# Two attention and two gated MLP layers on one core: gate and up weights copied inside DRAM into 4 KB rows and loaded from the copies

## The chip, the cores and the metric

The kernel runs on one core of one Trainium2 chip. The metric is the device time of one execution in microseconds (us), the median of several runs.

## The reference

Four layers are applied to one sequence x of 2048 tokens and 1024 features (bfloat16): attention, MLP, attention, MLP, each on a layer-normalised input and with its result added to x. Attention is linear, with 32 heads of 32 features. Cut to what matters:

```python
q, k, v = split(layernorm(x) @ wqkv)
phi = lambda t: where(t > 0, t + 1, exp(t)) + 1e-6
kv = einsum("bhsd,bhse->bhde", phi(k), v);  z = sum over tokens of phi(k)
x = x + ((phi(q) @ kv) / (phi(q) . z + 1e-6)) @ wo            # attention
gate, up = layernorm(x) @ W_gate, layernorm(x) @ W_up          # 1024 x 3584 each
x = x + ((gate * (gate > 0)) * up) @ W_down                    # MLP
```

## The kernel before

The tokens stand in 16 tiles of 128, in four quarters of four tiles. An attention layer (`layer_A`) goes through these stages on TensorE: projections to k and q, quarter by quarter (line 506; a unit is one token tile by 512 columns, eight matmuls of 128x512); the attention token products, in which phi(k) is multiplied with the tokens themselves (`m_products`, line 588); the small products with the value weights; and the output products (line 789). In the first layer, four quarters of projections take TensorE from 6 us to 104 us, and the token products follow until about 150 us.

Each projection unit writes one PSUM bank. ScalarE (lines 448 and 449) and VectorE (line 452, the join) empty it. The units rotate over a pool `ps` of four banks; in the first three quarters of layer 0 every third unit uses one of the two banks of `ps3`; in the last quarter only `ps` is used. A unit needs its token tile normalised by VectorE and transposed by a DMA (line 423, `xnT`), which the queue of SyncE (SP) issues.

Into the first layer's projections the kernel puts preparations for the MLP: 1 MB blocks of `W_down` are loaded (line 1218, tiles `wd`), VectorE makes four differences of each (line 1230), and SP stores them (line 1232, `td`).

An MLP layer (`layer_B`) runs in two chunks of 1024 tokens. Layers 1 and 3 are MLPs, so the chunks are (1,0), (1,1), (3,0), (3,1). Each chunk goes through 14 units u of 256 columns of `W_gate` ("g") and `W_up` ("u"). For each unit `load_gu` brings 128 partitions x 8 rows x 256 columns of bfloat16 of each of the two, so 1024 pieces of 512 bytes, 512 KB. Seven products instead of eight are made from blocks of them (line 1301). The differences of weight blocks that this takes are made in chunk (1,0) by `make_gu`, stored in DRAM as `tgu` in rows of 4 KB, and loaded again in the other three chunks (line 1202).

The weights go through a ring of five SBUF tiles (`_Ring`): a load is issued when the tile that it takes has come free. `_Later` holds jobs that are due at a count of steps (`later.at(delay, job)`); each unit of TensorE work is a step. Within blocks marked `manual_schedule` the named engines keep the order of the code. For all other engines a scheduler of the framework places each instruction, from its dependencies and its own estimate, so an instruction may stand on its queue far ahead of where the code names it. SP's queue is not among those named in the block that holds the token products (VectorE and GpSimd are).

SP issues its DMAs in order; an instruction that waits holds all that stand behind it. ScalarE's queue issues a few loads too, among them the first q weights in the first microseconds.

Of the kernel before, what the change touches and what calls it, by code (L numbers as in the profile page):

```python
# [11 lines left out]
BF16 = mybir.dt.bfloat16  # L12
F16 = mybir.dt.float16
PSUM = bass.MemoryType.PSUM
P = 128
NW = 512
# [7 lines left out]
class _Ring:  # L24


    def __init__(self, nc, slot, depth):
        self.nc, self.slot, self.depth = nc, slot, depth
        self.plan, self.tiles, self.loaded = [], {}, 0
# [63 lines left out]
class _Net:  # L93
    def __init__(self, tc, ctx, x_d, wqkv_d, wo_d, wg_d, wu_d, wd_d, out_d):
        nc = tc.nc
        self.tc, self.nc = tc, nc
        _, S, D = x_d.shape
        self.S, self.D = S, D
        self.ST, self.KT = S // P, D // P
        self.G = D // P  # L100
        self.F = wg_d.shape[1]
        self.FT = self.F // P
        self.NQ = self.ST // QT
        self.x_v = x_d.rearrange("b (st p) d -> p (b st) d", p=P)
        self.o_v = out_d.rearrange("b (st p) d -> p (b st) d", p=P)
        self.wqkv_v = wqkv_d.rearrange("(kt p) n -> p kt n", p=P)
        self.wo_v = wo_d.rearrange("(kt p) n -> p kt n", p=P)
        self.wgu_v = {"g": wg_d.rearrange("(kt p) f -> p kt f", p=P),
                      "u": wu_d.rearrange("(kt p) f -> p kt f", p=P)}
        self.wd_v = wd_d.rearrange("(u h p) n -> p h u n", p=P, h=2)  # L110
        self.U = self.F // (2 * P)

        pool = lambda name, bufs, **kw: ctx.enter_context(tc.tile_pool(name=name, bufs=bufs, **kw))
        self.const = pool("const", 1)
        self.xres = pool("xres", 1)
        self.big = pool("big", 16)
        self.ep = pool("ep", 7)
        self.small = pool("small", 4)
        self.ps = pool("ps", 4, space=PSUM)
        self.ps3 = pool("ps3", 2, space=PSUM)  # L120
        self.kvp = pool("kvp", 1, space=PSUM)


        self.spill = pool("spill", 1, space=bass.MemoryType.DRAM)
        self.NS = self.ST // 2
        self.ring = _Ring(nc, self.slot, 5)
        self.tgu = {(w, u): self.spill.tile([P, 4, NW], F16, name=f"t{w}{u}")
                    for w in "gu" for u in range(self.U)}
        self.td = self.spill.tile([P, 4, self.U, NW], F16, name="td")
        self.tw = {n: self.spill.tile([P, 8, NW], F16, name=f"t{n}") for n in ("q0", "q1", "k0", "k1")}  # L130
        self.dd = {p: self.spill.tile([P, 7, self.U // 2, NW // 2], F16, name=f"dd{p}") for p in self.DEEP}
        self.gi = {(m, u): self.spill.tile([P, 4, 2, 2, P], F16, name=f"gi{m}_{u}")
                   for m, first in ((5, 2), (6, 3)) for u in range(first, self.U - 1, 2)}
        self.inner = {}
        self.later = _Later()
        self.phi_lag = 0

        from concourse.masks import make_identity
        self.ident = self.const.tile([P, P], BF16, name="ident")
        make_identity(nc, self.ident[:, :])  # L140
        self.ones = self.const.tile([P, P], BF16, name="ones")
        nc.vector.memset(self.ones, 1.0)
        self.mean = 2.0 ** -11
        assert self.S == 2 ** 11
        self.eps6 = self.const.tile([P, 1], F32, name="eps6")
        nc.vector.memset(self.eps6, 1e-6)
        self.eps5 = self.const.tile([P, 1], F32, name="eps5")
        nc.vector.memset(self.eps5, 1e-5)
        self.xall = self.xres.tile([P, self.ST, D], F32, name="x")
        self.x = [self.xall[:, t, :] for t in range(self.ST)]  # L150
        self.acc = self.const.tile([P, 2 * self.ST], F32, name="acc")

        self.xb = [x[:, D // 2:D].bitcast(BF16) for x in self.x]
        self.xnT, self.xn, self.pk, self.slabs, self.xs = {}, {}, {}, {}, {}
        self.away = [self.spill.tile([P, D], F32, name=f"away{t}") for t in range(self.ST)]
# [324 lines left out]
    def layer_A(self, l, last_ln):  # L480
# [34 lines left out]
        def k_unit(q, j, c, between=None):  # L515
            t = q * QT + j
            pk = self.pk_home(l, t)
            self.phi(project(f"k{c}", q, j, between), pk[:, c * NW:(c + 1) * NW])
            later.at(1 + (10 if self.phi_lag else 0), lambda: k_sum(t, slice(c * NW, (c + 1) * NW)))
# [126 lines left out]
        def q_unit(sc, j, c, lag=None):  # L646
            if c == 0 and (sc, j) not in pq_of:
                a = self.slot(f"pq{l}_{sc}", [P, QT, D])
                for i in range(QT):
                    pq_of[sc, i] = a[:, i, :]  # L650
            pq = pq_of[sc, j]
            self.phi(project(f"q{c}", sc, j), pq[:, c * NW:(c + 1) * NW])
            if c == H - 1 and lag is not None:
                later.at(lag, lambda: z_mult(sc, j))
# [212 lines left out]
        def column_major(f, q):  # L867
            return [lambda j=j, c=c: f(q, j, c) for c in range(H) for j in range(QT)]
# [33 lines left out]
        if l == 0:  # L902
            first = self.head_units(lambda *a: k_unit(0, *a), lambda *a: q_unit(0, *a), *steps)
        else:
            first = column_major(k_unit, 0)
# [10 lines left out]
        else:  # L916
            run(first)
            k = iter(row_major(k_unit, 1))
# [22 lines left out]
        with self.tc.manual_schedule(engines={mybir.EngineType.DVE, mybir.EngineType.Pool}):  # L941
            q3 = row_major(q_unit, self.NQ - 1)
            out0 = column_major(out_unit, 0)
            bring = self.bring_back if l else self.load_x
            ring.load_to(ring.index((l, "v1")) + 1)
            m_products(q3.pop(0))
            q3.insert(0, lambda: None)
            later.at(1, lambda: self.behind(ring.last, bring, range(self.NS)))
            for t in range(self.NS, self.ST - QT, 2):
                later.at(10 + t, lambda t=t: self.behind(self.last_turn, bring, (t, t + 1)))  # L950

            def with_fold(u, i):
                return lambda: (u(), fold_wo(i // 2) if i % 2 == 0 else None)

            run(q3[:2])
            run([with_fold(u, i) for i, u in enumerate(q3[2:] + out0[:1])])
            run(out0[1:3])
            ring.free_slowly((l, "o0"), later, 2)
            for i in range(11, self.ST):
                later.at(1 + 3 * (i - 11), lambda i=i: z_mult(*divmod(i, QT)))  # L960
            self.ln_later(last_ln, 0, 2, 2, 2)
            run(out0[3:])
            for sc in range(1, self.NQ - 1):
                if sc == 1:
                    for j in range(QT):
                        self.ln_at(2 * j + 2, last_ln, QT + j, 2)
                        later.at((11 if l else 12, 13, 15, 16)[j], lambda j=j: self.sums_x(last_ln, 0, j))
                if sc == 2 and l:
                    for j in range(QT):
                        later.at(11 + j, lambda j=j: q_turn(self.NQ - 1, j))  # L970
                    for t in range(self.ST - QT, self.ST):
                        later.at(3 + t, lambda t=t: self.behind(self.last_turn, bring, (t,)))
                if sc == 1 and l == 0:
                    for w, n in (("g", 3), ("u", 11)):
                        later.at(n, lambda w=w: self.behind(
                            self.last_x, lambda w: self.make_gu(ring.get((last_ln, 0, w, 0)), w, 0), (w,)))
                run(row_major(out_unit, sc))
            self.pairs = out_pairs(self.NQ - 1)
            self.turns = [] if l else [lambda j=j: q_turn(self.NQ - 1, j) for j in range(QT)] + [
                lambda t=t: self.behind(self.last_turn, bring, (t,)) for t in range(self.ST - QT, self.ST)]  # L980
# [213 lines left out]
    def sums_gu(self, t):  # L1194
        return t[:, 4:8, :].bitcast(F16).rearrange("p t (k f) -> p t k f", f=P)

    def load_gu(self, t, w, u, first, d):
        self.nc.sync.dma_start(out=self.raw_gu(t),
                               in_=self.wgu_v[w][:, :, u * 2 * P:(u + 1) * 2 * P])
        if not first:  # L1200
            b = slice(1, 4, 2) if 6 in d else slice(5 in d, 4)
            self.nc.sync.dma_start(out=t[:, 4:8, :][:, b, :].bitcast(F16), in_=self.tgu[w, u][:, b, :])
# [609 lines left out]
```

## Time and profile before

| | |
|---|---|
| median of 3 runs | 1438.24 us (1438.23 to 1438.44) |
| profiled execution, its own time | 1439.99 us |
| its span, first to last instruction | 1437.9 us |
| TensorE (PE) matmul busy | 1427.1 us, 99% |
| VectorE (DVE) / ScalarE (ACT) / GpSimd (POOL) busy | 1045.2 / 623.3 / 309.3 us |
| queue of SP: bytes, share of 16 DMA engines | 313.57 MB, 73.1% |
| loads of gate and up weights | 56 + 56, 512 KB each |

The profiled execution is 1.75 us above the median, and 2.1 us of it lie around its span. The busy time of PE is a model (matmuls overlap their ends), so waits of PE are read from the idle time before its instructions. The DMA share is the mean busy share of the core's 16 DMA engines. Packets of one engine overlap a little, so a saturated stretch shows a share above 1. The granted clock was 1.000 over the span.

### The profile page before, as it was taken

To read this page: it belongs to the slowest core of one execution; us is meant where nothing else is said; L and a number is where in the kernel's file an instruction comes from. 1 tells how busy PE (TensorE), PEld (TensorE's weight loads), DVE (VectorE), ACT (ScalarE), POOL (GpSimd) and SP (SyncE) were. 2 spreads that over 40 slices of the span, in tenths; PEclk is the share of its full clock that TensorE was granted. 3 is DMA by queue.
4 is the path that set the end of the run, shared out by engine and by line. 5 is a ranking of instruction groups with operands and counts; after the bars stand their busy time and mean duration, and the time that the engine had idled before them with its cause. 6 is when DMAs were issued, how large, how long until landed. Compare 5 with 4: busy or idle time off the path is not lost.

```text
span 1437.9 us, 21394 instructions
## 1 busy us (share of the span) xinstructions
PE 1427.1 (99%) x7720; PEld 739.7 (51%) x7748; DVE 1045.2 (73%) x2013; ACT 623.3 (43%) x1143; POOL 309.3 (22%) x220
## 2 busy tenths in 40 slices
PE   9999999999999999999999999999999999999998
PEld 4444444444455444545654444445554565555557
DVE  7978698778685666558778886866766864766895
ACT  7872564333325244332058725733443433444301
POOL 1453860010100011110032477510111011111102
PEclk9999999999999999999999999999999999999999
DMA  9950787898559999966983218998878699975575
GB/s 286 240 162 8 172 209 202 278 335 288 200 192 294 323 367 345 291 216 199 302 277 93 70 22 234 287 274 262 268 225 294 228 304 335 274 229 174 193 260 183
DMA packets 367865, 337.74 MB, mean 235 GB/s; under 512 B 110032, under 2 KB 327760, under 8 KB 366736
## 3 DMA queue, kind: packets, MB, share of 16 engines
q1 hardware_dynamic: 359184, 313.57, 73.1%
q10 hardware_dynamic: 7136, 18.88, 3.4%
q0 software_dynamic: 1440, 3.93, 0.7%
q8 instruction: 60, 0.98, 0.3%
q14 instruction: 45, 0.37, 0.1%
HBM read 246.87 MB, written 64.82 MB: 217 GB/s over the span
## 4 chain that ended last, share of the span: by engine, by line
PE 91%; DVE 3%; DMA 2%; ACT 2%; SPq 1%; issue 1%; ACTq 0%; DVEq 0%
PE ps L506 11%; PE yu L1301 9%; PE yg L1301 9%; PE xg L1301 6%; PE xu L1301 6%; PE dy L1447 6%; PE dx L1447 5%; PE i L1154 5%; PE ps L789 4%; PE zu L1301 3%; PE zg L1301 3%; PE my L588 3%; PE dyT L1489 2%; PE mv L588 2%; PE mx L588 2%; PE dy L1489 2%
## 5 line engine op out<-in xcount | busy, mean ns | idle before, releaser
L1301 PEld LDWEIGHTS <-w 128*128 128x128 f16 (+1 forms) x2768 | 270.4, 98 | 297.2 <-issue 4.6
L506 PE MATMUL ps<-w,xnT 128*128 128x512 bf16 x768 | 169.9, 380 | 0.6 <-ACT xnT L361 0.2
L1381 POOL TENSOR_TENSOR h<-m5u,m5g 128x512 f16<-128x512 f32 x28 | 37.1, 1326 | 425.3 <-DVE m5u L1377 252.5
L506 PEld LDWEIGHTS <-xnT 128*128 128x128 bf16 x768 | 74.4, 98 | 90.3 <-issue 1.8
L1301 PE MATMUL xg<-xnT,w 128*128 128x512 f16 x448 | 115.5, 379 | 0.0
L1301 PE MATMUL xu<-xnT,w 128*128 128x512 f16 x448 | 115.0, 380 | 0.0
L1489 PEld LDWEIGHTS <-h 128*128 128x128 f16 x1008 | 98.6, 98 | 12.9
L1381 POOL TENSOR_TENSOR h<-c22u,c22g 128x512 f16<-128x512 f32 x28 | 36.0, 1285 | 289.8 <-DVE c22u L1377 247.8
L1447 PEld LDWEIGHTS <-h 128*128 128x128 f16 x616 | 60.3, 98 | 71.8 <-issue 0.3
L1301 PE MATMUL yu<-s,w 128*128 128x512 f16 x376 | 96.5, 379 | 0.5 <-DVE zu L1357 0.5
L1301 PE MATMUL yg<-s,w 128*128 128x512 f16 x376 | 96.9, 379 | 0.0
L449 ACT ACTIVATE e<-e,eps 128x512 f32<-128x512 f32 x128 | 91.0, 720 | 3.2
L736 POOL TENSOR_TENSOR kvc<-pq,kvc 128x1024 f32<-128x1024 bf16 x32 | 78.5, 2452 | 53.1 <-DVE den L741 32.8
L789 PE MATMUL ps<-T,pqT 128*128 128x512 bf16 x374 | 83.0, 380 | 0.5
L1328 DVE TENSOR_TENSOR h<-yu,r 128x512 f16<-128x512 f32 x56 | 38.6, 690 | 53.8 <-PE yu L1301 53.8
L1325 ACT ACTIVATE r<-yg 128x512 f32<-128x512 f32 x56 | 33.4, 597 | 101.3 <-PE yg L1301 101.3
L527 POOL TENSOR_TENSOR kvc<-kvc,slab 128x512 f32<-128x512 f32 x46 | 57.2, 1249 | 75.9 <-DVE slab L452 72.7
L1447 PE MATMUL dx<-w,h 128*128 128x512 bf16 x327 | 72.5, 380 | 0.5
L448 ACT ACTIVATE e<-ps 128x512 f32<-128x512 f32 x92 | 54.2, 590 | 28.4 <-PE ps L506 27.9
L1154 PEld LDWEIGHTS <-x 128*128 128x128 f16 x504 | 49.3, 98 | 33.5 <-issue 1.9
L1325 ACT ACTIVATE r<-zg 128x512 f32<-128x512 f32 x56 | 32.9, 587 | 76.7 <-PE zg L1301 76.7
L748 POOL TENSOR_TENSOR pq<-pq,den 128x1024 bf16<-128x1024 bf16 x32 | 61.1, 1909 | 6.8 <-DVE den L743 6.8
(286 smaller groups left out, 2630.6 us busy)
## 6 DMA issues: line engine op xcount, KB each, us to landing
w<-in_B_W_gate_dram SPq DMA_DIRECT2D x56, 512.0 KB, 6.4
w<-in_B_W_up_dram SPq DMA_DIRECT2D x56, 512.0 KB, 6.0
w<-ddT SPq DMA_DIRECT2D x21, 896.0 KB, 6.4
w<-td SPq DMA_DIRECT2D x18, 896.0 KB, 5.0
w<-dd SPq DMA_DIRECT2D x18, 896.0 KB, 5.9
x<-away SPq DMA_DIRECT2D x30, 512.0 KB, 7.5
away<-x SPq DMA_DIRECT2D x24, 512.0 KB, 8.1
w<-in_B_W_down_dram SPq DMA_DIRECT2D x12, 896.0 KB, 6.1
```

What stands on the lines that cost most here:

```text
L449: self.last_exp = nc.scalar.activation(out=e, in_=e, func=ACT.Exp, scale=-1.0, bias=self.eps6[:, 0:1])
L506: nc.tensor.matmul(by_row(ps), lhsT=self.xnT[l, l_q][:, kt, j * P:(j + 1) * P], rhs=w[:, kt, :].rearrange("p (b i d) -> p i b d", i=R, d=H ...
L588: nc.tensor.matmul(banks[j], lhsT=A(i)[:, j * P:(j + 1) * P], rhs=B(i), start=start and i == 0, stop=i == NS - 1, skip_group_check=True)
L736: nc.gpsimd.tensor_tensor(out=prod, in0=pq_of[sc, j], in1=zrow, op=ALU.mult)
L748: nc.gpsimd.tensor_tensor(out=heads(pq), in0=heads(pq), in1=den[:, :].unsqueeze(2).to_broadcast([P, D // HD, HD]), op=ALU.mult)
L789: nc.tensor.matmul(ps, lhsT=pqT[sc][:, g, j * P:(j + 1) * P], rhs=T[g // 4][:, g % 4, n2 * NW:(n2 + 1) * NW], start=(g == 0), stop=(g == G ...
L1154: nc.tensor.matmul(b[:, w, :], lhsT=B[p][:, w, k, :], rhs=A[p][:, k, :], start=start and w == 0 and k == 0, stop=k == 1, skip_group_check= ...
L1301: nc.tensor.matmul(ps, lhsT=W[w][m][:, k, :], rhs=A[m][:, k, :], start=start and k == 0, stop=k == 3, skip_group_check=True)
L1325: self.last_relu = nc.scalar.activation(out=out, in_=ps, func=ACT.Relu)
L1381: nc.gpsimd.tensor_tensor(out=h[:, 3, :], in0=V["u"], in1=V["g"], op=ALU.mult)
L1447: nc.tensor.matmul(banks[j], lhsT=A(k)[:, j * P:(j + 1) * P], rhs=w[:, i, :], start=start and k == 0, stop=k == self.U - 1, skip_group_che ...
L1489: nc.tensor.matmul(out, lhsT=A[i // 2][:, i % 2, j * P:(j + 1) * P], rhs=B[m][:, i, :], start=start and i == 0 and j == 0, stop=i == NK - ...
```

## The change

Each of the 28 blocks of gate and up weights gets a tile `wc` in DRAM, and `lay_again` issues one DMA from DRAM to DRAM for it on SP's queue: 1024 pieces of 512 bytes are read at the stride of the weight matrix and written one behind the other, so that a partition's eight pieces make one row of 4 KB. The calls stand at the start of the token products: units 0 to 6 in layer 0, units 7 to 13 in layer 2. `load_gu` takes the copy where the code has already named it, except for the first two units of chunk (1,0): that is units 2 to 6 in chunk (1,0), units 0 to 6 in (1,1), and all 14 in (3,0) and (3,1), 80 of the 112 loads. The other loads are as before.

```diff
+        self.wc = {(w, u): self.spill.tile([P, 4, NW], BF16, name=f"c{w}{u}")
+                   for u in range(self.U) for w in "gu"}
+        self.relaid = set()
...
             ring.load_to(ring.index((l, "v1")) + 1)
+            self.lay_again(range(self.U // 2, self.U) if l else range(self.U // 2), 1, 2)
             m_products(q3.pop(0))
...
+    def lay_again(self, units, first, step):
+
+        def lay(w, u):
+            self.nc.sync.dma_start(out=self.wc[w, u][:, :, :].rearrange("p a (b f) -> p (a b) f", f=2 * P),
+                                   in_=self.wgu_v[w][:, :, u * 2 * P:(u + 1) * 2 * P])
+            self.relaid.add((w, u))
+
+        for n, u in enumerate(units):
+            for k, w in enumerate("gu"):
+                self.later.at(first + (2 * n + k) * step, lambda w=w, u=u: lay(w, u))
+
     def load_gu(self, t, w, u, first, d):
-        self.nc.sync.dma_start(out=self.raw_gu(t),
-                               in_=self.wgu_v[w][:, :, u * 2 * P:(u + 1) * 2 * P])
+        if (w, u) in self.relaid and not (first and u < 2):
+            self.nc.sync.dma_start(out=t[:, 0:4, :], in_=self.wc[w, u][:, :, :])
+        else:
+            self.nc.sync.dma_start(out=self.raw_gu(t),
+                                   in_=self.wgu_v[w][:, :, u * 2 * P:(u + 1) * 2 * P])
```

The order of matmuls on PE and of the work on GpSimd is the same in both kernels. On VectorE a few rows near 50 us change places, on ScalarE four. SP's queue has 28 DMAs more, and the scheduler puts them as follows. The first place is the head of SP's queue, while the first token tiles are loaded, normalised and transposed (`w` with a number: weights of the projections; `xnT_0`, `xnT_1`: transposed tokens of the first and second quarter). Before:

```order
L463 DMA x<-in_A_x_dram 128x1024
L40 DMA w_176<-in_A_wqkv_dram 128x4x512
L463 DMA x<-in_A_x_dram 128x1024
L423 DMA_TRANSPOSE xnT_0_189<-x 128x8x128 x2
L463 DMA x<-in_A_x_dram 128x1024 x10
L423 DMA_TRANSPOSE xnT_1_439<-x 128x8x128
```

And in the changed kernel, from the last of these loads of x on (`cg`, `cu`: the copies of gate and up blocks):

```order
L466 DMA x<-in_A_x_dram 128x1024
L1204 DMA cg_109<-in_B_W_gate_dram 1024x1x256
L1204 DMA cu_110<-in_B_W_up_dram 1024x1x256
L1204 DMA cg_111<-in_B_W_gate_dram 1024x1x256
L1204 DMA cu_112<-in_B_W_up_dram 1024x1x256
L426 DMA_TRANSPOSE xnT_0_217<-x 128x8x128
L1204 DMA cg_113<-in_B_W_gate_dram 1024x1x256
L426 DMA_TRANSPOSE xnT_0_217<-x 128x8x128
L466 DMA x<-in_A_x_dram 128x1024 x10
L1204 DMA cu_114<-in_B_W_up_dram 1024x1x256
L1204 DMA cg_115<-in_B_W_gate_dram 1024x1x256
L1204 DMA cu_116<-in_B_W_up_dram 1024x1x256
```

Five copies stand ahead of the loads of x that the second quarter needs, and eight ahead of its first transposition. The second place is further down SP's queue, at the last block of `W_down` that the first layer's projections prepare (`wd_1111` before, `wd_1139` after). Before:

```order
L423 DMA_TRANSPOSE xnT_3_883<-x 128x8x128 x2
L1218 DMA wd_989<-in_B_W_down_dram 128x4x1024
L1232 DMA td<-wd_840 128x2x512 x4
L423 DMA_TRANSPOSE xnT_3_883<-x 128x8x128 x2
L1232 DMA td<-wd_989 128x2x512 x4
L1218 DMA wd_1111<-in_B_W_down_dram 128x4x1024
L40 DMA w_1222<-in_A_wqkv_dram 128x8x512
```

And in the changed kernel:

```order
L426 DMA_TRANSPOSE xnT_3_911<-x 128x8x128 x2
L1250 DMA td<-wd_1017 128x2x512 x4
L1204 DMA cu_126<-in_B_W_up_dram 1024x1x256
L1204 DMA cg_127<-in_B_W_gate_dram 1024x1x256
L1204 DMA cu_128<-in_B_W_up_dram 1024x1x256
L1204 DMA cg_129<-in_B_W_gate_dram 1024x1x256
L1204 DMA cu_130<-in_B_W_up_dram 1024x1x256
L1204 DMA cg_131<-in_B_W_gate_dram 1024x1x256
L1204 DMA cu_132<-in_B_W_up_dram 1024x1x256
L1204 DMA cg_133<-in_B_W_gate_dram 1024x1x256
L1236 DMA wd_1139<-in_B_W_down_dram 128x4x1024
L40 DMA w_1250<-in_A_wqkv_dram 128x8x512
```

Of the 28 copies, those of layer 2 included, 25 stand ahead of this last `wd` load: 17 ahead of the third block of `W_down`, eight between the stores of the fourth and the load of the fifth. The last three come behind it, ahead of the transpositions of q at 140 us.

## The prediction

> **What bounds the kernel now.** I read the page first, then the work by stage.
>
> ```profile
> span 1437.9 us, 21394 instructions
> PE 1427.1 (99%) x7720; PEld 739.7 (51%) x7748; DVE 1045.2 (73%) x2013; ACT 623.3 (43%) x1143; POOL 309.3 (22%) x220
> ```
> ```profile
> 0.00:20.00 20.00, 17.95 (x85) 7.84 (x86) 13.17 (x31) 12.34 (x25) 3.84 (x10) 1.00 0.87 268
> 1420.00:1437.90 17.90, 13.98 (x129) 12.28 (x126) 6.59 (x12) 1.24 (x3) 3.99 (x6) 1.00 0.21 64
> ```
>
> (The second fence: stretch, its length, busy time of PE, weight loads, DVE, ACT and POOL, granted clock, DMA share, GB/s.) PE is idle for 1437.9 - 1427.1 = 10.8 us. Of these 2.05 lie in the first 20 us and 3.9 in the last 18, where no gate or up load is waited for, so at most 4.8 us are left for all waits on loads in the MLPs. The longest of them:
>
> ```profile
> 469.90 6.20 DMA xnT<-xnb
> 491.65 9.00 DMA w<-tu
> ```
> ```profile
> 479.52 1.02 PE L1301 MATMUL vg<-s,w 128*128 128x512 f16 x4 [0.35 <-DVE x L1460]
> 500.69 0.61 PE L1301 MATMUL vu<-s,w 128*128 128x512 f16 x2 [1.11 <-DMA w<-tu]
> ```
>
> The first two rows are the chain of waits at the start of chunk (1,1): it runs through a transposition that takes 6.2 us to land and a weight load that takes 9.0 us, both behind a full queue. The other two are what PE lost there, 0.35 and 1.11 us.
>
> Next comes the stage into which the copies go.
>
> ```profile
> 0.00:91.30 91.30, 89.25 (x416) 40.13 (x417) 74.91 (x137) 70.59 (x135) 29.52 (x30) 1.00 0.87 248
> 5.00:10.00 5.00, 4.30 (x30) 2.08 (x30) 4.25 (x11) 2.63 (x8) 0.00 (x0) 1.00 1.08 359
> 105.00:140.00 35.00, 34.89 (x162) 15.84 (x162) 28.84 (x74) 12.01 (x20) 11.55 (x5) 1.00 0.00 1
> 9.05 51.33 PE L506 MATMUL ps<-w,xnT 128*128 128x512 bf16 x237
> ```
>
> From 9 us on PE runs without a wait, and the DMAs that feed it are at a share of 0.87 over 91 us, where 1.08 is a full queue. The idle DMA time comes later: 35 us at a share of 0.00 under the token products. The queue order shows that the copies don't stand there, but in the first 91 us.
>
> **The change: the later loads.** 80 loads of 512-byte pieces become loads of 4 KB rows. Prices of 512 KB:
>
> ```profile
> DMA packets 2065, 1.04 MB, mean 346 GB/s; under 512 B 35, under 2 KB 2065, under 8 KB 2065
> q1 hardware_dynamic: 2065, 1.04, 114.8%
> ```
> ```profile
> q10 hardware_dynamic: 7136, 18.88, 3.4%
> ```
>
> The first fence is the DMA view from 327 to 330 us, nearly all pieces of 512 bytes: 1.04 MB in 3 us, so 1.5 us for 512 KB, or 3 x 1.148 / 2 = 1.72 us of packet time. The second is ScalarE's queue over the whole run, mostly 4 KB rows: 3.4% of 1437.9 us for 18.88 MB gives 1.36 us of packet time. A load saves 0.36 us, the 80 save 29 us of DMA time. On the path lies only what PE waits for: five raw loads of chunk (1,1) stand ahead of the one that PE waits for at 500.7 us, 5 x 0.36 = 1.8, more than the 1.11 us lost; the wait at 479.5 loses its 0.35 too. I take -1.5 us, between 0 and -4.8. They are covered otherwise: PE never waits in the rest of the chunks, and nothing is late next, since the queue gets shorter.
>
> **The change: the price of a copy.** No row shows DRAM to DRAM. From below: a copy moves the same 1024 pieces by the same engines as a raw load, 1.5 us. From above: reading and writing one after the other, each at that price, 3.0 us, and waits between them may put it at 3.3. The nearest row is the load, but it has only half of a copy's traffic with DRAM; I take 2.4, a little above the middle, and keep 1.5 and 3.3 as the ends. A gain is excluded: 28 DMAs that were not there take time in a queue.
>
> The Trainium skill, "DMA: Bandwidth & Descriptors", section "Latency and other measured facts", gives 207 to 214 GB/s in each direction for copies between HBM tensors in rows of 16 KiB at their full rate. My estimate from that page is 524 KB / 214 = 2.45 us for a copy, with which the sum below would be 1 us higher. No run here shows it yet.
>
> **The change: what waits.** The copies are issued without a wait, as SP reaches them, and all DMAs run on the same 16 engines, in the order of issue: the rows of ScalarE's first weight loads show it.
>
> ```profile
> L40 ACTq DMA_DIRECT2D w<-in_A_wqkv_dram x2: 388/454/520, 7.4 to 7.9; - x2
> DMA to landing us min/median/max: 5.9/6.4/6.9
> ```
>
> They hold the first q weights and land 5.9 and 6.9 us after their issue, at 14.8 us at the latest, behind what SP issued before. So a copy issued by SP delays everything issued later. Four stations, each against the time at which PE used it before (units of 1.73 us from 9.05):
>
> 1. q weights: four copies ahead, 14.8 + 4 x 2.4 = 24.4, used from 15.1: 9 us late.
> 2. First transposition of the second quarter:
>
> ```profile
> L423 SPq DMA_TRANSPOSE xnT<-x x1: 1237/1237/1237, 27.3 to 27.3; - x1
> DMA to landing us min/median/max: 4.2/4.2/4.2
> ```
>
> It lands at 31.5 and is used by the 17th unit, at 35.0. Eight copies make 19.2, some 2 us of them in idle DMA time: 48.7, 14 us late.
>
> 3. Third block of `W_down`, 17 copies. VectorE works in order, and its sums of the block stand between the joins that empty PSUM banks.
>
> ```profile
> L1218 SPq DMA_DIRECT2D wd<-in_B_W_down_dram x1: 411/411/411, 60.6 to 60.6; - x1
> DMA to landing us min/median/max: 2.5/4.1/5.7
> 72.08 0.68 DVE L1230 TENSOR_TENSOR wd<-wd 128x1024 f16<-128x1024 bf16 x1
> ```
>
> It lands at 66.3; the copies add 40.8 less about 7 of idle time: 100. VectorE wants it at 72.1, and PE can go on for some 5 us with the banks it has: 23 us late.
>
> 4. Last block, 25 copies:
>
> ```profile
> L1218 SPq DMA_DIRECT2D wd<-in_B_W_down_dram x1: 380/380/380, 85.2 to 85.2; - x1
> DMA to landing us min/median/max: 6.1/6.1/6.1
> 97.58 0.68 DVE L1230 TENSOR_TENSOR wd<-wd 128x1024 f16<-128x1024 bf16 x1
> 98.70 0.69 DVE L452 SCALAR_TENSOR_TENSOR slab<-ps,e 128x512 bf16<-128x512 f32 x1 [0.44 <-ACT e L449]
> 93.66 10.52 PE L506 MATMUL ps<-w,xnT 128*128 128x512 bf16 x48
> ```
>
> It lands at 91.3. The copies add 25 x 2.4 = 60. Idle DMA time that can take them: 91.3 x (1 - 0.87 / 1.08) = 17.8, less 2 in which the first loads are only starting, so 15.7. Landing at 91.3 + 60 - 15.7 = 135.6. Room: VectorE's sum began 6.3 us after the landing (97.58). The join behind it ended at 99.4 and frees the bank that the last unit takes (four banks in the last quarter, so the unit from 95.4 hands its own to the one from 102.3): 2.9 us more. PE is late by 135.6 - 91.3 - 9.2 = 35 us. The four stations are one growing delay, so the largest counts, not the sum; per microsecond of a copy's price it moves by 25 us: 13 us at 1.5, 50 at 3.0, 58 at 3.3. What is behind has no room to recover, since PE has no other slack, and nothing to lose: the last three copies run into the empty stage.
>
> Moved rows on VectorE and ScalarE (a few, near 50 us) I cost at nothing: they lie inside a stage that waits for DMAs. PE may need to warm up after the last long wait:
>
> ```profile
> 1.35 3.78 PE L302 MATMUL idle<-e 128*128 128x512 bf16 x10 [1.35 <-DVE e L299]
> ```
>
> Ten matmuls at the start took 3.78 us, at 10.52 / 48 = 0.22 each they would take 2.2: 1.6 us more; I take +1, between 0 and 2.
>
> The sum on the profiled execution: 1439.99 + 35 - 1.5 + 1 = 1474.5; on the median, 1.75 lower, **1473 us**.
>
> **The rivals.**
>
> *Copies as cheap as a load* (1.5 to 2.0 us). For it: packets, engines and sizes are those of the load row. Against: DRAM takes twice the bytes. 13 to 26 us late: 1451 to 1464; at the load's own price 1438.2 + 13 - 0.5 = 1451.
>
> *Copies dearer than 3.3 us.* For it: small pieces on both sides, while the loads and transpositions that they meet want the same engines; SP also holds copies behind `td` stores that wait for VectorE, which leaves DMA time unused. Against: the stores of this trace land no later than loads. At 4 us each, 25 x 4 - 24.9 = 75 late: 1513.
>
> *The other side: the copies hide.* If packets between DRAM and DRAM ran beside the traffic to SBUF instead of in its queue, no landing of the first 91 us would move, and only the shorter loads would show: 1436.7, no change that can be told; all 4.8 us of waits gone, 1433. It decides below (15.7 + 9.2) / 25 = 1.0 us for a copy, 520 GB/s. For it: the total of the DMA time is there, in the empty 35 us and behind. Against: no stretch shows more than about 375 GB/s, and the q weights did wait for their turn.
>
> **How the numbers follow.** Copies of 2.0 to 3.3 us: 0.55, 1464 to 1495, likeliest 1473. Cheap copies: 0.24, 1451 to 1464. Dear ones: 0.15, 1495 and up. Hidden: 0.06, of which a third is a gain beyond 0.2%. A difference of 0.2% (2.9 us) is about what a measurement can tell here. The range 1451 to 1502 leaves out the hidden case and most of the dear one, 0.2 together. Faster 0.02, same 0.04, slower 0.94.
>
> **What the changed profile would show.** The DMA share of the first four slices near full, and still high at 100 to 130 us, where it was 0.00. First wait of PE near 14 us, for a load of projection weights; then more at transposed tokens; VectorE idle for tens of us in all before line 1248 (the old 1230), for DMAs of `wd`. Packets of 512 bytes fewer by 80 x 1024 and more by 28 x 1024. After 150 us the same course as before, shifted, with the wait at 500.7 gone. It is wrong if PE's busy share in the first 105 us stays at 99%, or if the last `wd` lands before 110 us.

## The result, and the profile after

The changed kernel takes 1461.43 us (median of 5 runs, 1461.32 to 1464.61), the kernel before, run beside it, 1438.29 us (median of 5, 1438.23 to 1438.74). The ratio is 1.0163, with a 95% interval from 1.0152 to 1.0175: 23.1 us slower. The profiled execution of the changed kernel took 1461.43 us too.

The head of its page:

```profile
span 1459.7 us, 21454 instructions
...
PE 1435.6 (98%) x7748; PEld 741.4 (51%) x7748; DVE 1045.0 (72%) x2013; ACT 624.1 (43%) x1143; POOL 309.3 (21%) x220
...
DMA packets 325305, 352.42 MB, mean 241 GB/s; under 512 B 110480, under 2 KB 274960, under 8 KB 324176
```

PE's busy time grew by 8.5 us, though its matmuls are the same: part of this is 28 records that the trace of before lacks (x7720 there), most of it matmuls at half clock, below. The packets fell from 367865 by 42560. Worked out, 80 loads with 128 pieces in place of 1024, and 28 copies of 1024, make 43008 fewer: the loads do come from the copies.

What PE waited for, in the changed kernel (its longest waits; us in total, times, longest):

```profile
PE ps L509 <- DVE slab L455: 6.8, 1, 6.8
PE ps L509 <- DMA xnT<-x: 5.0, 1, 5.0
PE ps L509 <- DVE pq L455: 3.2, 3, 2.1
PE idle L305 <- DVE e L302: 1.4, 1, 1.4
PE ps L509 <- DMA w<-in_A_wqkv_dram: 1.0, 1, 1.0
PE ps L509 <- DMA td<-wd: 0.8, 1, 0.8
```

All but the fourth, which was there before, stand at line 509, the old 506: the projections of the first layer. They make 16.8 us. The rows that name VectorE's joins (line 455) are waits for PSUM banks, and so in effect is the last, put down to a store: VectorE's join behind the fourth block of `W_down` ended at 96.86 us, and PE went on at 96.92. VectorE itself stood in front of blocks of `W_down`:

```profile
DVE wd L1248 <- DMA wd<-in_B_W_down_dram: 21.4, 4, 10.3
```

The last of these loads, in the changed kernel, between 113 and 123 us:

```profile
L1236 SPq DMA_DIRECT2D wd<-in_B_W_down_dram x1: 1763/1763/1763, 113.1 to 113.1; - x1
...
  DVE wd L1248: 10.3, 1
...
DMA to landing us min/median/max: 9.4/9.4/9.4
```

Issued at 113.1, it landed at 122.4; before it was issued at 85.2 and landed at 91.3. So it came 31.1 us later, and VectorE waited 10.3 us for it. The stages of the changed kernel (columns as in the prediction):

```profile
0.00:91.30 91.30, 81.43 (x363) 35.66 (x364) 63.87 (x123) 62.74 (x121) 22.28 (x25) 0.96 1.09 297
...
24.00:26.00 2.00, 2.00 (x5) 0.69 (x6) 0.00 (x0) 0.00 (x0) 0.00 (x0) 0.50 1.19 327
...
105.00:140.00 35.00, 28.20 (x123) 12.34 (x121) 20.08 (x40) 16.36 (x26) 11.07 (x9) 0.90 0.77 231
...
140.00:160.00 20.00, 20.00 (x95) 9.04 (x94) 16.64 (x46) 5.64 (x10) 6.30 (x2) 1.00 0.00 1
```

The DMA share of the first 91.3 us went from 0.87 to 1.09, a full queue; in the stretch that was empty it is 0.77, until the copies are done. The second row shows the rest of the loss: behind the wait of 5.0 us PE ran at a granted clock of 0.50. Such stretches, behind the waits of 5.0, 2.1 and 6.8 us, cost another 6.1 us: against the kernel before, profiled once more (`b_again` below), PE's lateness grows from 5.77 to 8.23, from 10.50 to 12.18 and from 21.12 to 23.09 us behind them, while it waits for nothing. With the 16.8 that is 22.9 us. PE ends 23.1 late, but it was 0.5 us ahead of `b_again` before the first of these waits, so 23.6 are to be explained: each of the six longest waits at line 509 cost PE 0.1 to 0.2 us more than its own length.

One more row for the place where all of it has come together, the first token products (`b_again`, then the changed kernel):

```profile
L588 PE MATMUL mx<-slab,x x64: 379/379/379, 104.5 to 118.1; 128*128 128x512 bf16 x64
```
```profile
L591 PE MATMUL mx<-slab,x x35: 379/379/634, 127.3 to 134.9; 128*128 128x512 bf16 x35
```

PE begins them 22.8 us late, the output products 23.1 late, and ends the kernel 23.1 late. Nothing was lost or won after 130 us.

### The profile page after: what moved, and what is told of

It is laid out like the page before. It is cut to its first block, busy times and chain, and to the rows that moved or that the text cites. A ratio compares the mean times of both kernels' runs of the same rounds, so it can differ in the third digit from the quotient of the medians.

```text
span 1459.7 us, 21454 instructions
## 1 busy us (share of the span) xinstructions
PE 1435.6 (98%) x7748; PEld 741.4 (51%) x7748; DVE 1045.0 (72%) x2013; ACT 624.1 (43%) x1143; POOL 309.3 (21%) x220
## 4 chain that ended last, share of the span: by engine, by line
PE 88%; DVE 5%; DMA 3%; ACT 2%; SPq 1%; issue 1%; DVEq 0%; ACTq 0%
PE yu L1319 9%; PE yg L1319 9%; PE dy L1465 7%; PE ps L509 7%; PE xg L1319 6%; PE xu L1319 6%; PE dx L1465 5%; PE i L1158 5%; PE ps L792 4%; PE zu L1319 3%; PE zg L1319 3%; PE my L591 3%; DMA wd<-in_B_W_down_dram 2%; PE dyT L1507 2%; PE mx L591 2%; PE mv L591 2%
## 5 line engine op out<-in xcount | busy, mean ns | idle before, releaser
L509 PE MATMUL ps<-w,xnT 128*128 128x512 bf16 x768 | 176.7, 388 | 17.1 <-DVE slab L455 6.8
L509 PEld LDWEIGHTS <-xnT 128*128 128x128 bf16 x768 | 75.6, 100 | 111.9 <-issue 21.8
```

Source lines behind the costliest of these rows:

```text
L509: nc.tensor.matmul(by_row(ps), lhsT=self.xnT[l, l_q][:, kt, j * P:(j + 1) * P], rhs=w[:, kt, :].rearrange("p (b i d) -> p i b d", i=R, d=H ...
```

## Experiments

The lateness of PE, read from the traces by the start of the same matmul, is the common measure. "Unit n" is the n-th projection unit of the first layer, counted from 0 (it has 56 before the token products); the reference is `b_again`. (That execution lost 0.5 us at its very start, hence the numbers below nought.) The last column is the difference of the medians to the kernel before, run on the same chip; the profiled execution was not always the median (1450.33 us for `e4_half`, where the median is 1449.13, and 1462.64 for `e2_copies_only`, where it is 1464.62).

| kernel | copies ahead of the last `wd` | unit 8 | unit 40 | unit 54 | unit 55 | output products | end | measured |
|---|---|---|---|---|---|---|---|---|
| changed | 25 | 8.2 | 8.2 | 14.2 | 21.1 | 23.1 | 23.1 | +23.1 |
| e1_behind | 0 | -0.3 | -0.2 | -0.2 | -0.2 | -0.2 | 0.4 | +0.1 |
| e2_copies_only | 25 | 8.1 | 8.1 | 15.9 | 21.8 | 23.4 | 24.3 | +26.0 |
| e3_eighth | 28 of 64 KB | 4.5 | 5.9 | 5.9 | 5.9 | 5.9 | 6.1 | +6.0 |
| e4_half | 14 | 8.0 | 10.2 | 11.9 | 11.9 | 11.9 | 12.0 | +10.5 |
| e5_last11 | 17 | 7.4 | 8.2 | 16.8 | 16.8 | 16.8 | 16.9 | +16.3 |
| e7_first5 | 5 | 9.1 | 9.1 | 9.1 | 9.1 | 9.1 | 9.5 | +9.8 |
| e8_eight | 8, the last ones | 0.1 | 0.1 | 0.1 | 3.6 | 5.3 | 6.2 | +6.1 |

The theory: the price is a copy's time in the DMA queue, ahead of a load that an engine working in order waits for. The rivals: SP's issuing is the price; or copies slow down whatever runs beside them.

**All copies behind the last load of the stage.**

```diff
-                self.later.at(first + (2 * n + k) * step, lambda w=w, u=u: lay(w, u))
+                self.later.at(first + (2 * n + k) * step, lambda w=w, u=u: self.behind(self.ring.last, lambda u: lay(w, u), (u,)))
```

> The same 28 copies and the same 80 loads from them, but each copy is held on SP's queue until the last weight load of the token products (v1) has been issued: in layer 0 the copies of units 0 to 6 then stand behind the last W_down load, those of units 7 to 13 behind the same load of layer 2. Theory (a copy costs its time in the DMA queue where an in-order engine waits for a load behind it): the first 105 us go as in the kernel before, without a wait of PE, and only the shorter loads are left, 1.5 us: about 1436.8 us, ratio 0.998 to 1.000; the wait of 1.11 us before line 1301's unit near 500 us is gone. Rival (copies disturb whatever runs beside them, by contention for DRAM or the DMA engines, wherever they stand): 28 x 1.85 = 52 us of copying slow down the token products or the transpositions of q behind them, and a good part of the 23 us stays: 1445 to 1460.

Measured: 1438.79 us against 1438.65, ratio 0.9999 (0.9991 to 1.0008). The whole loss is gone with the same copies and the same loads. The stretch of the token products in this kernel:

```profile
105.00:140.00 35.00, 35.00 (x164) 15.88 (x163) 28.59 (x74) 12.19 (x21) 11.55 (x6) 1.00 0.69 198
```

The DMAs are at 0.69 there, and PE is busy all of the 35 us: traffic of copies by itself takes nothing from it. That disposes of contention under the token products. For the first 130 us of the changed kernel it is argued from the account above: waits and half clock make up the loss, and leave nothing for matmuls slowed in another way. The expected gain of 1.5 us did not come; in its place one wait is new:

```profile
PE fold L775 <- DMA w<-in_A_wo_dram: 0.9, 1, 0.9
```

It lies in layer 2, where the last copy and the transpositions stand around the load of the output weights. But it is 0.9, not 1.5, and the next two experiments show what became of the gain.

**The copies alone.** As the change, without `self.relaid.add((w, u))`, so that all 112 loads are raw.

> The copies stand exactly where the change has them, but nothing is loaded from them: all 112 loads of gate and up weights are raw, in pieces of 512 bytes. The difference to the changed kernel is what the 4 KB rows bring by themselves. Theory: 1.5 to 1.8 us, the waits of 0.35 and 1.11 us at the start of chunk (1,1) and a little more, so 1461.4 + 1.6 = 1463.0 us. Rival (the shorter loads bring more, and the copies cost more than 23 us): 1465 us and up. Rival (the loads were never in PE's way, and what the changed kernel won later has another source): 1461.4.

Measured: 1464.62 us, ratio 1.0181 (1.0167 to 1.0195), an interval that overlaps that of the change. By the traces PE loses 0.9 us in chunks (1,1) and (3,0), a wait of 0.44 us at 523 us among it, which the changed kernel doesn't lose. That this is the work of the 4 KB rows is not shown: `b_again`, whose loads are raw too, doesn't lose it either. The medians are 2.8 us apart in their differences to the kernel before; where that comes from is not settled.

**The kernel before, once more.** Its file is unchanged.

> The kernel before, unchanged, profiled once more. It asks whether PE's two waits at the start of chunk (1,1), 0.35 and 1.11 us, and the lag of 1.75 us of the profiled execution behind the median belong to the kernel or to that one execution. Theory (to the one execution: in every later trace with raw loads PE lost less there): no wait above 0.5 us there, span near 1436.2 us, time near 1438.3. Rival (to the kernel, and the later kernels win it by the shorter loads): both waits again, span 1437.9, time 1440.0.

Measured: 1438.65 us, in one run. Its span, its busy times and PE's longest waits:

```profile
span 1436.5 us, 21422 instructions
...
PE 1428.3 (99%) x7748; PEld 739.9 (52%) x7748; DVE 1045.3 (73%) x2013; ACT 623.5 (43%) x1143; POOL 309.3 (22%) x220
```
```profile
PE idle L302 <- DVE e L299: 1.4, 1, 1.4
PE tp L351 <- DVE centred L344: 0.7, 1, 0.7
PE yu L1301 <- DVE zu L1357: 0.5, 1, 0.5
```

Neither the 1.11 us at `vu<-s,w` nor the 0.35 at `vg<-s,w` is there. They belonged, as far as a second execution can show, to the one that the prediction read, which was 1.75 us above the median. Of 15 runs of the kernel before beside the first four experiments the fastest took 1438.05 us and the slowest 1439.90.

**An eighth of each copy.**

```diff
-            self.nc.sync.dma_start(out=self.wc[w, u][:, :, :].rearrange("p a (b f) -> p (a b) f", f=2 * P),
-                                   in_=self.wgu_v[w][:, :, u * 2 * P:(u + 1) * 2 * P])
-            self.relaid.add((w, u))
+            self.nc.sync.dma_start(out=self.wc[w, u][:, :, :].rearrange("p a (b f) -> p (a b) f", f=2 * P)[:, 0:1, :],
+                                   in_=self.wgu_v[w][:, 0:1, u * 2 * P:(u + 1) * 2 * P])
```

> All loads raw, and each of the 28 copies moves an eighth: 128 pieces of 512 bytes, 64 KB. The scheduler puts these small copies still earlier, 16 ahead of the first transposition and all 28 ahead of the first W_down load, so their place is no better than in the change. Theory (the copy's time in the DMA queue is the cost): 28 copies move as much as 3.5 whole ones, 28 x 1.85 / 8 = 6.5 us, plus a fixed part of each; the idle DMA time in the first 91 us takes this, so the last W_down block decides nothing, and only the wait at the first tokens, a few us, and its warm-up stay: 1439 to 1445 us. Rival (SP's issue, and its holding of each copy until an earlier DMA has landed, is the cost): 28 more DMAs hold SP as often as before, and most of the 23 us stays, 1455 us and up.

Measured: 1444.66 us, ratio 1.0043 (1.0028 to 1.0058), at the upper end of what the theory gave and far from the rival's 1455: what a copy moves is most of its price. What is left of the loss is SP's part, and most of it arises at the head. The first transposition that PE waited for, in this kernel:

```profile
L426 SPq DMA_TRANSPOSE xnT<-x x1: 1367/1367/1367, 17.6 to 17.6; - x1
...
  PE ps L509: 2.9, 1
...
DMA to landing us min/median/max: 3.3/3.3/3.3
```

It was quick (3.3 us), but was issued at 17.6, against 12.7 before: 13 small copies stood ahead of it, each with some 0.6 us on SP and more where SP held it. PE's wait of 2.9 us for it and the slow matmuls behind make 4.9 of the 6 us that this kernel loses. So SP's issuing has a price of its own where much is issued at once.

**Layer 0's copies alone in their places.** The 14 of layer 2 are put behind `ring.last` in layer 2 (as in the first experiment), the others are left to the scheduler.

> As the change, but only layer 0's 14 copies stand where the scheduler put them, all ahead of the third W_down block; the 14 of layer 2 are held back to the token products of layer 2. Loads from copies as in the change. Theory (one growing delay, the largest station counts): at the last W_down block 14 x 1.85 = 25.9 us of copying meet 15.2 us of idle DMA time and 9.5 us of room, so about 1 us of lateness there; the larger is then the station at the first tokens, 5.4 + 1.35 us of waits and 2.6 us of slow matmuls, and at the third W_down block 5 us more at most; less 1.5 for the loads: 1446 to 1452 us, +8 to +14. Rival (each copy costs PE the same, wherever it stands): half of 23.2, 1450 and PE's waits spread evenly. Rival (the last block decides alone): +1 - 1.5, 1438.

Measured: 1449.13 us, ratio 1.0073 (1.0059 to 1.0087), within the range of the theory. PE is 8.0 us late behind the first tokens, 10.2 behind the second `W_down` block and 11.9 behind the fourth; nothing is added at the last (unit 54 and unit 55 are equally late). The third block, where the theory put up to 5 us, added nothing: VectorE waited for the first, second and fourth. "Half of 23" predicts the time as well, but not this: two thirds of it are lost at the first tokens.

**The last eleven behind the last block.**

```diff
+            self.gate = self.gate if l else ring.last
             self.lay_again(range(self.U // 2, self.U) if l else range(self.U // 2), 1, 2)
...
-                self.later.at(first + (2 * n + k) * step, lambda w=w, u=u: lay(w, u))
+                self.later.at(first + (2 * n + k) * step, (lambda w=w, u=u: self.behind(self.gate, lambda u: lay(w, u), (u,)))
+                              if 2 * u + k > 16 else (lambda w=w, u=u: lay(w, u)))
```

> The change, but its last 11 copies are held back until the last W_down block and the weights behind it have been issued; the first 17 stand where they stood. The same copies run in the same stage of PE, and the DMA queue is as full; only what stands behind them differs. Theory (the delay comes from an in-order engine that waits for a load behind the copies): the changed kernel's last wait of 7.2 us and its slow matmuls vanish, and what was lost up to the third W_down block stays: PE 14.65 us late at the token products, 1438.3 + 14.65 = 1453 us. At the last block 17 x 1.85 = 31.5 less 15.2 of idle DMA time less 9.5 of room make 6.8, less than that. Rival (the copies slow PE by traffic beside it): PE late by 20 us or more, 1459 us and up.

Measured: 1454.97 us, ratio 1.0121 (1.0097 to 1.0145). The wait of 6.8 us is gone:

```profile
PE ps L509 <- DVE pq L455: 6.2, 4, 4.7
PE ps L509 <- DMA xnT<-x: 4.7, 1, 4.7
```

The two that remain are the first tokens and the third block (with the fourth). The lateness behind these blocks came to 16.8, not 14.65. Up to the stores of the fourth block the changed kernel, this one and `e2_copies_only` have one order on SP, and were 14.2, 16.8 and 15.9 late: that much differs from one execution to the next where the queue is full.

**The first five alone at the head.** The same edit with `> 4` for `> 16`.

> The change, but only its first five copies stay at the head of SP's queue; the other 23 are held back until the last W_down block has been issued, and run under the token products. Theory: PE loses 1.35 and 5.4 us at the first tokens and some 2 us of slow matmuls behind them, 8.7 us as in the changed kernel, and nothing after: 1447 us. 23 x 1.6 to 1.85 = 37 to 43 us of copying begin near 113 us and end by 156, before the output weights are wanted near 170. Rival (the loss at the head is made good later, since PE's lateness gives the DMAs time): under 1443. Rival (23 copies in a row are too many for the token products, and the transpositions of q or the output weights come late): a wait of PE near 165 to 175 us, 1450 and up.

Measured: 1448.42 us, ratio 1.0071 (1.0055 to 1.0087). PE's longest waits:

```profile
PE ps L509 <- DMA xnT<-x: 5.7, 1, 5.7
PE idle L305 <- DVE e L302: 1.4, 1, 1.4
PE ps L509 <- DMA w<-in_A_wqkv_dram: 1.0, 1, 1.0
PE fold L775 <- DMA w<-in_A_wo_dram: 0.8, 1, 0.8
```

PE is 9.1 us late behind the first tokens (8.7 was expected) and nothing of it comes back; the copies under the token products cost nothing there. The 0.8 us in layer 2, as in the first experiment, was not foreseen.

**Eight copies right ahead of the last block.** The stores `td` are kept in a list; the eight copies `cu_126` to `cg_133` are put behind the fourth block's last store, the other 20 behind `self.gate`.

> Only the eight copies that stand between the fourth block's stores and the last W_down load stay ahead of it, as in the change; the other 20 are held back until that load and the weights behind it have been issued. It asks when idle DMA time can be set against copies. Theory 1 (only the idle time behind a copy's issue counts, and SP reaches these eight near 85 us, with the last load due right behind): 8 x 1.87 = 15 us less 9.5 us of room, so PE waits some 5 us for the last block, and about 2 us of slow matmuls follow: 1445 us. Theory 2 (as the prediction reckoned, all idle DMA time up to the landing counts, wherever it lies: 15.2 us): 15 - 15.2 - 9.5 is below nothing, no wait: 1438.5 to 1439. Rival (what matters is the copies' place right ahead of the load, not their sum): PE late by 10 us or more, 1449 and up.

Measured: 1444.65 us, ratio 1.0040 (1.0025 to 1.0054), near the 1445 of theory 1. Of the lateness 5.3 us arise at the last block; 0.9 came at 703 us, with a wait of 0.7 for a load of stored differences (`td`) that was not foreseen. The last load of `W_down` and PE's longest wait in this kernel:

```profile
L1237 SPq DMA_DIRECT2D wd<-in_B_W_down_dram x1: 1921/1921/1921, 95.6 to 95.6; - x1
...
DMA to landing us min/median/max: 9.2/9.2/9.2
```
```profile
PE ps L509 <- DVE slab L455: 3.4, 1, 3.4
```

It lands at 104.8, 13.3 us later than the 91.5 of `b_again`, and PE is 3.5 us late for it: the room is 9.8. So the idle DMA time of 0 to 80 us is of no use to copies that are issued from 83 us on. In the changed kernel the copies were issued from 6 us on and, by the working below, found nearly all of it.

**The price by the size of the pieces.** 28 copies of 512 KB with pieces of 4 KB on both sides, in the places of the first experiment, and all loads raw:

```diff
-            self.nc.sync.dma_start(out=self.wc[w, u][:, :, :].rearrange("p a (b f) -> p (a b) f", f=2 * P),
-                                   in_=self.wgu_v[w][:, :, u * 2 * P:(u + 1) * 2 * P])
-            self.relaid.add((w, u))
+            self.nc.sync.dma_start(out=self.wc[w, u][:, :, :],
+                                   in_=self.wqkv_v[:, u % 8, 0:4 * NW].rearrange("p (a n) -> p a n", a=4))
```

> A price: 28 copies of 512 KB from DRAM to DRAM in pieces of 4 KB on both sides (128 pieces, taken from the projection weights), in the places where the held copies of pieces of 512 bytes ran without a cost to PE; nothing is loaded from them, and all loads are raw. Theory (a copy's price is that of a load of the same pieces, with little on top): under 1.4 us from landing to landing against 1.6 (layer 0) and 1.87 us (layer 2) for the pieces of 512 bytes; 1438.5 us. Rival (DRAM's traffic, twice that of a load, sets the price): no difference, 1.6 to 1.9 us. Rival (copies between DRAM tensors run at 207 to 214 GB/s at best): 2.45 us.

Measured: 1438.32 us, in one run. Three stretches in which nearly only copies ran: the changed kernel from 105.5 to 116.5 us, `e7_first5` from 120 to 150, both with pieces of 512 bytes, and this kernel from 825 to 842:

```profile
DMA packets 6035, 3.05 MB, mean 277 GB/s; under 512 B 96, under 2 KB 6031, under 8 KB 6035
```
```profile
DMA packets 16397, 8.29 MB, mean 276 GB/s; under 512 B 253, under 2 KB 16395, under 8 KB 16395
```
```profile
DMA packets 1484, 5.37 MB, mean 316 GB/s; under 512 B 172, under 2 KB 172, under 8 KB 1484
```

524 KB at 276 GB/s are 1.90 us for a copy in small pieces, and at 316 GB/s 1.66 us in 4 KB pieces; from landing to landing it is 1.87 and 1.62 in layer 2 (`e1_behind` and this kernel, 12 steps each). In layer 0, where a few loads run among the copies, it is 1.82 and 1.72. All three expectations missed: the size of the pieces counts, but takes off a seventh at most, less than the quarter that the theory wanted and more than the nothing of the first rival. The second rival is the figure that the prediction quoted from the Trainium skill, "DMA: Bandwidth & Descriptors", section "Latency and other measured facts", 207 to 214 GB/s; here copies run at 276 and 316 GB/s in each direction, and the measurement decides.

## Why the prediction was right, and where it was not

1473.0 us was forecast, in a range from 1451 to 1502, and slower with 0.94. It is slower, and the range holds 1461.4. The likeliest case was 11.6 us too high; the case that came is the prediction's first rival, copies as cheap as a load, to which it gave 0.24 and 1451 to 1464.

- **Where the copies act.** Right. PE loses its time before 130 us, at the first tokens, at the third and fourth and at the last `W_down` block, because of where the scheduler put the copies. `e1_behind` takes the place away and leaves the rest, and the loss is gone.
- **The price of a copy.** This is the term that was mis-sized: 2.4 us taken, 1.87 measured (1.82 to 1.91 by the stretch; where the copies run among much else, as in the first 91 us, no row shows it alone). The bounds, 1.5 and 3.3, held; the value between them was chosen by the doubled traffic with DRAM, and the traces show a copy at 1.25 times the load (276 GB/s against the 346 of the prediction's row), not at 1.6. At 25 copies that is 25 x 0.53 = 13 us. With 1.87 the fourth station gives 25 x 1.87 - 15.7 - 9.2 = 21.9 us; PE's last unit was 21.1 late.
- **Idle time and room.** 15.7 and 9.2 us were reckoned. Against `b_again` (91.5) the landing moved by 30.9, so 25 x 1.87 - 30.9 = 15.8 us of copying went into idle time, if the price was 1.87 there too; the room is 30.9 - 21.1 = 9.8, as in `e8_eight`. That all the idle time of 91 us could be used is no rule: it held here, where the copies were spread over the stage, and `e8_eight` shows where it doesn't.
- **The four stations.** That they are one growing delay of which the largest counts is what the table shows: 8.2, then 14.2, then 21.1. Their sizes were 9, 14, 23 and 35. The first came out near its number by luck: the loads of q weights cost 1.0 us only, since SP held the third and fourth copy at 9 and 12 us and ScalarE's loads went ahead; but the same hold delayed the transposition behind them, and PE waited 5.0 us for that. "In the order of issue" also doesn't hold from one queue to the other: SP's first two copies, issued at 5.9 and 6.6 us, landed at 15.4 and 17.5, ScalarE's q weights, issued at 7.4 and 7.8, at 14.0 and 16.1. The second station never showed, since PE was already 8.2 us late there. At the third, 17 x 1.87 gives 14 us; the block landed at 87.8, and PE was 10.5 late for it. The 14.2 came about by 1.7 us of slow matmuls and 2.0 at the fourth block, for which VectorE waited 2.7 us: a station that the prediction doesn't have.
- **Warm-up.** 1 us was taken, between 0 and 2. Behind the last wait it was 2.0. It also came behind the waits of 5.0 and 2.1 us, 2.5 and 1.7, inside the delay that then counted. The prediction had only one such stretch.
- **The shorter loads.** -1.5 us was wrong; it is 0. The step read two waits in one execution as if the kernel had them, and then took 1.75 us off for the median, which by `b_again` is free of these same waits: they were subtracted twice. What the 4 KB rows would bring in an execution that does lose there was not measured.
- **The sum with these terms**: 1438.3 + 21.1 + 2.0 = 1461.4. That it meets the median to a tenth is luck, since the lateness is measured against one execution, of 1438.65 us.
- **What the profile would show.** The full queue in the first 91 us, the work at 100 to 130 us, VectorE's waits before line 1248 (21.4 us), the count of packets and the same course after 150 us are there. The prediction's "no stretch shows more than about 375 GB/s", an argument against copies that hide, was a little low: the trace of before reaches 386 from 165 to 170 us. The first wait of PE came at 15 us, for a load of projection weights as forecast.

No version here beats the kernel before. In `b_again` PE is idle for 8.2 us in all (1436.5 less 1428.3), and none of its longest waits is for a load of gate and up weights: shorter loads have nothing to win there.

## What to carry to other kernels

An added DMA is paid for where an in-order engine waits for something behind it in the queue: find its place in the issue order, not in the code, and hold it behind the last load that is wanted; here the same 28 copies cost 23.1 us in one place and nothing that could be told behind the last load (layer 0's from 102 us on, layer 2's from 815). Count idle DMA time only from the moment at which the transfer is issued. Before a wait of a microsecond is booked as a gain, profile the kernel before a second time, and don't correct from one execution to the median for waits that you have subtracted already.

## What the runs showed of the hardware

- PE's clock fell to half after a short wait. In the changed kernel PE stood still for 2.1 us before 89.1 us, and then:

```profile
87.00:89.10 2.10, 0.01 (x1) 0.00 (x0) 1.33 (x3) 1.32 (x2) 0.00 (x0) 1.00 1.08 45
89.10:91.00 1.90, 1.88 (x8) 0.88 (x8) 1.87 (x4) 0.00 (x0) 0.00 (x0) 0.84 1.12 282
91.00:93.00 2.00, 2.00 (x7) 0.63 (x6) 1.19 (x2) 1.32 (x2) 1.47 (x1) 0.50 0.98 230
93.00:95.00 2.00, 2.00 (x9) 0.87 (x8) 0.16 (x1) 0.55 (x1) 0.00 (x0) 0.80 1.04 364
```

The granted clock stays at 1.00 for 1.3 us after PE has gone on, and is 0.50 from 90.4 to 93.8 us. All changes of the clock between 20 and 130 us of this trace, at 22.12, 28.95, 90.39, 93.80, 121.11 and 127.93 us, lie 3.41 us or a multiple of it apart, as if fixed windows of this length decided. Two such windows follow. The first is the one that ended at 90.39 us in the changed kernel. The second is of `e4_half`, where the clock is at half from 24.49 to 27.9 us; it began two windows before 24.49:

```profile
86.98:90.39 3.41, 1.30 (x7) 0.58 (x6) 2.59 (x5) 1.32 (x2) 0.00 (x0) 1.00 1.07 119
```
```profile
17.66:21.08 3.42, 1.48 (x7) 0.49 (x5) 0.69 (x1) 2.87 (x5) 2.41 (x3) 1.00 1.18 294
```

Behind the first, with PE busy for 1.30 us, the clock is at half; behind the second, with 1.48, it stays at 1.00 in the next 3.41 us. So here the busy time within one window decided, and not the length of a wait; this is inferred from a few windows. The Trainium skill, "TensorE: Matmul & The Clock Gate", section "What's actually happening", puts the half rate after at least one idle window of about 3.4 us; the length of the stretch, 3.4 us, agrees with such a window, and the wait that was enough here, 2.1 us, doesn't fill one.

- A copy from DRAM to DRAM in 512-byte pieces costs 1.87 us per 512 KB where little else runs, a quarter more than a load of the same pieces (1.5 us by the prediction's row), though it makes twice the traffic with DRAM; in 4 KB pieces it costs 1.62.
